# Sub-chunk outputs written from PSUM into x^T, and who issues the six small transfers

## The chip, the cores and the metric

One core of one Trainium2 chip runs the whole program. The metric is the device time of one execution in microseconds (us): the median of three runs is 731.37 us (729.12 to 733.59). Engines are called as in the profile: PE (TensorE), PEld (its weight loads), DVE (VectorE), ACT (ScalarE), POOL (GpSimd), SP (SyncE, which here only issues DMAs).

## The reference, cut to what matters

```python
def _attn_ref(r, k, v, w, u):                  # (4, 8, 768, 48): batch, heads, tokens, D
    state = np.zeros((B, H, D, D))
    for t in range(S):
        cur = np.einsum('bhd,bhe->bhde', u[None] * kt, vt)
        y[:, :, t] = np.einsum('bhd,bhde->bhe', rt, state + cur)
        state = w[None, :, :, None] * state + np.einsum('bhd,bhe->bhde', kt, vt)
    return y
x = attn_out.transpose(0, 2, 1, 3).reshape(3072, 384)
x = (np.maximum(x @ w_in, 0) ** 2) @ w_out     # 384 -> 2048 -> 384
h = x @ w2_in                                  # 384 -> 1024
# h * softmax(h), layer norm over the 1024, times g_ln, then @ w2_out (1024 -> 384)
```

## The kernel before, in words

The 3072 tokens are 24 chunks of 128, and six blocks of 512 tokens (four chunks each) go through the first two matrices. The attention is computed chunk by chunk. Chunks 0 to 3 are the first of their batch and take a direct form. Chunks 4 to 23 are worked in two sub-chunks of 64 tokens: `prep_rk`, `prep_b`, `prep_kt` scale r and k, `pe_scores` and `pe_u` multiply on PE, `dve_mask` and `dve_state` put the masked scores and the state beside v and r, and `pe_av` gives the chunk's output.

`pe_av` (L505 to L526) leaves the output in one PSUM bank as y: a pair of heads has one head in partitions 0 to 47 and the other in 64 to 111, and the four pairs lie one after another, 128 columns each. The next matrix wants x^T as three tiles of 128 full partitions. So x^T (`xr`) takes pairs 0 to 2 in the same partitions, and the fourth pair is cut into pieces of 16 rows that fill the gaps, partitions 48 to 63 and 112 to 127, of the three tiles. Before the change ACT copies all of y into the SBUF tile `ys` (L519), and SP issues eight transfers from `ys` to `xr` a chunk: two of 48 partitions by 384 columns (L524), six of 16 partitions by 128 columns (L526). `split_x` then makes a high part `xh` on ACT (L570) and a low part `xl` on DVE (L571), both float32r, of the chunk's columns of its block.

The block's work is a list of steps. `p1(i)` (L651 to L659) multiplies 128 columns of w_in with x^T, nine matmuls, and ACT applies relu, square and the rounding to `gh` (L656, L657, L658), DVE takes the remainder `gl` (L659). `p2(i)` (L669 to L673) multiplies both with w_out, nine matmuls. `p1` is written two steps ahead of `p2`; `gh` and `gl` have three buffers, and the PSUM of `p1` has two.

Chunks 4 to 7 are the second block's chunks. Their attention is put between the steps of the first block (the `side` lists), and there the weights are still being made: `w1_conv` takes a loaded piece, turns its 64-bit numbers into 32 bits on DVE (L591, L594, L597), rounds it on ACT (L609, `wih` or `woh`) and takes the remainder on POOL (L610, `wil` or `wol`), and `w1_load` asks SP for the next piece (L580, L582). The chunks from 8 on are put between the steps of the later blocks (the `ev` lists). The second network follows, token tile by token tile.

SP's queue holds, in one order, the loads of chunks (L241 to L246), the weight loads, the eight transfers a chunk, and stores. A DMA that waits holds what is behind it. The order of instructions on each engine is made by the tile scheduler, which simulates the program in time; only the small matmuls marked with `pin` keep the written order. `xr` has two buffers, `ys` one. The tag of `ys` is also used once for the table `dup` before chunk 4.

Of the kernel before, what the change touches and what calls it, by code (L numbers as in the profile page):

```python
# [8 lines left out]
F32 = mybir.dt.float32  # L9
# [7 lines left out]
B, H, S, D = 4, 8, 768, 48  # L17
NP = H // 2
DM = H * D
KD = DM // 128  # L20
NT = B * S
C = 128
# [4 lines left out]
GR = 112  # L27
# [150 lines left out]
def rwkv_moe_moe2_kernel(ctx, tc, rkd, tok, tk2, wd, w, u, w_in, w_out, w2_in, w2_out, g_ln, out):  # L178
    nc = tc.nc
# [16 lines left out]
    ap = att_ctx.enter_context(tc.tile_pool(name="ap", bufs=2))  # L196
# [212 lines left out]
    def pin(ins):  # L409

        tc.keep_in_program_order(ins)
# [94 lines left out]
    def pe_av(c, yb=2):  # L506
        rk_t.pop(c)
        tok_t.pop(c)
        y = ps[:, yb, :].rearrange("p (a i) -> p a i", a=NP)
        for s in range(2):  # L510
            i = slice(s * CH, (s + 1) * CH)
            for p in range(NP):
                for j in range(2):
                    pin(nc.tensor.matmul(  # L514
                        y[64 * j:64 * j + D, p, i], vs[c % 2][:KR[j], j, s, p], mv[c % 2][:KR[j], j, p, i],
                        start=True, stop=True,
                    ))
        ys = ap.tile([GR, NP, C], F32, tag="ys", bufs=1, name="ys")
        nc.scalar.copy(ys, y[:GR])  # L519
        xr = ap.tile([128, KD, C], F32, tag="xr", name="xr")  # L520
        xr_t[c] = xr
        for j in range(2):
            o = 64 * j
            nc.sync.dma_start(out=xr[o:o + D], in_=ys[o:o + D, 0:KD])  # L524
            for k in range(KD):
                nc.sync.dma_start(out=xr[o + D:o + 64, k], in_=ys[o + 16 * k:o + 16 * k + 16, KD])  # L526

    def pe_av_direct(c, yb=2):

# [359 lines left out]
    for q, c in enumerate(range(4, 8)):  # L889
        t = 5 + 3 * q + (q > 0)  # L890
        side[t].append(lambda c=c: (prep_rk(c), put_state(c, 0), prep_kt(c), prep_b(c)))
        side[t + 1].append(lambda c=c: (pe_u(c), pe_scores(c), dve_state(c), dve_mask(c)))
        side[t + 2].append(lambda c=c: (pe_av(c, 0), load_chunk(c + 2)))
        side[t + 3].append(lambda c=c: split_x(c))
# [20 lines left out]
    for q, t in enumerate(visits):  # L915
        c = 2 * B + q
        if q:
            ev[t].append(lambda c=c: pe_av(c - 1))
            ev[t + 2].append(lambda c=c: split_x(c - 1))
        if c < NC:  # L920
            ev[max(t - 2, first_full)].append(
                lambda c=c: (prep_rk(c), put_state(c, 0), prep_kt(c), prep_b(c))
            )
            ev[t].append(lambda c=c: (pe_u(c), pe_scores(c), dve_state(c), dve_mask(c)))
        if q and c + 1 < NC:
            ev[t].append(lambda c=c: load_chunk(c + 1))
# [114 lines left out]
```

## Time and profile before

| | |
|---|---|
| median of three runs | 731.37 us (729.12 to 733.59) |
| the profiled execution: time, span | 732.05 us, 730.3 us |
| PE busy | 702.9 us (96%) |
| DVE, ACT, POOL busy | 418.7 us (57%), 321.7 us (44%), 267.9 us (37%) |
| mean granted clock of TensorE | 0.993 |

The span is from the first to the last instruction of the profiled execution. Busy time is time in which an engine has an instruction at work; issuing DMAs and waiting for semaphores are not counted. A granted clock of 1.0 is full speed. A busy share is a mean over stages: the start, where weights are made, and the later blocks differ much.

### The profile page before, as it was taken

To read this page: it belongs to the slowest core of one execution; us is meant where nothing else is said; L and a number is where in the kernel's file an instruction comes from. 1 tells how busy PE (TensorE), PEld (TensorE's weight loads), DVE (VectorE), ACT (ScalarE), POOL (GpSimd) and SP (SyncE) were. 2 spreads that over 40 slices of the span, in tenths; PEclk is the share of its full clock that TensorE was granted. 3 is DMA by queue.
4 is the path that set the end of the run, shared out by engine and by line. 5 is a ranking of instruction groups with operands and counts; after the bars stand their busy time and mean duration, and the time that the engine had idled before them with its cause. 6 is when DMAs were issued, how large, how long until landed. Compare 5 with 4: busy or idle time off the path is not lost.

```text
span 730.3 us, 13143 instructions
## 1 busy us (share of the span) xinstructions
PE 702.9 (96%) x5088; PEld 599.7 (82%) x5088; DVE 418.7 (57%) x752; ACT 321.7 (44%) x625; POOL 267.9 (37%) x297
## 2 busy tenths in 40 slices
PE   3799999999999999999999999999999999999996
PEld 3588768788888888888888888888899999999996
DVE  7799986444534334433333266614768767777671
ACT  1444645454554554555454455634433232322232
POOL 6969777444533333334222022802303030300000
PEclk9999999999999999999999999999999999999999
DMA  8956552222312222321161016221111100000001
GB/s 277 267 200 212 140 179 79 89 67 85 106 57 89 67 66 66 108 65 60 41 202 35 12 41 202 88 86 34 66 65 49 40 22 11 22 22 22 22 34 38
DMA packets 35113, 62.73 MB, mean 86 GB/s; under 512 B 7777, under 2 KB 17378, under 8 KB 35042
## 3 DMA queue, kind: packets, MB, share of 16 engines
q1 hardware_dynamic: 35042, 61.80, 27.2%
q8 instruction: 42, 0.69, 0.4%
q14 instruction: 29, 0.24, 0.1%
HBM read 48.41 MB, written 9.44 MB: 79 GB/s over the span
## 4 chain that ended last, share of the span: by engine, by line
PE 86%; DMA 7%; SPq 2%; POOL 2%; ACT 1%; issue 1%; DVE 0%; ACTq 0%; POOLq 0%; DVEq 0%
PE ps L651 9%; PE ps L653 8%; PE ps L652 8%; PE ps L670 8%; PE ps L669 8%; PE ps L673 8%; PE ps L819 5%; PE ps L818 5%; PE ps L821 5%; PE ps L755 5%; PE ps L757 5%; PE ps L756 5%; DMA stg<-in_w_out_dram 3%; PE ps L802 3%; PE ps L514 2%; PE ps L437 2%
## 5 line engine op out<-in xcount | busy, mean ns | idle before, releaser
L659 DVE TENSOR_TENSOR gl<-ps,gh 128x512 fp32r<-128x512 f32 (+1 forms) x100 | 66.7, 668 | 168.2 <-ACT gh L658 166.9
L651 PE MATMUL ps<-xh,wih 128*128 128x512 f32 (+1 forms) x300 | 117.5, 393 | 1.8 <-ACT xh L570 1.0
L653 PE MATMUL ps<-xh,wil 128*128 128x512 f32 (+1 forms) x300 | 115.2, 385 | 2.3 <-POOL wil L610 2.3
L669 PE MATMUL ps<-gh,woh 128*128 128x512 f32 (+1 forms) x300 | 113.3, 383 | 2.2 <-ACT gh L658 2.1
L652 PE MATMUL ps<-xl,wih 128*128 128x512 f32 (+1 forms) x300 | 115.0, 384 | 0.1
L670 PE MATMUL ps<-gh,wol 128*128 128x512 f32 (+1 forms) x300 | 113.3, 383 | 0.0
L656 ACT ACTIVATE ps<-ps 128x512 f32<-128x512 f32 (+1 forms) x100 | 56.3, 564 | 115.9 <-PE ps L653 115.4
L356 POOL TENSOR_TENSOR mv<-mv,pt 48x512 f32<-48x512 f32 x40 | 52.1, 1302 | 93.0 <-DMA mv<-in_rkd_dram 92.3
L673 PE MATMUL ps<-gl,woh 128*128 128x512 f32 (+1 forms) x300 | 83.3, 382 | 0.0
L653 PEld LDWEIGHTS ps<-xh,wil 128*128 128x128 f32 x300 | 56.7, 189 | 14.3 <-POOL wil L610 3.1
L651 PEld LDWEIGHTS ps<-xh,wih 128*128 128x128 f32 x300 | 56.4, 189 | 14.5 <-ACT xh L570 1.6
L669 PEld LDWEIGHTS ps<-gh,woh 128*128 128x128 f32 x300 | 56.0, 189 | 13.9 <-ACT gh L658 2.9
L652 PEld LDWEIGHTS ps<-xl,wih 128*128 128x128 f32 x300 | 56.8, 190 | 10.8 <-DVE xl L571 0.6
L818 PE MATMUL ps<-w2oh,lth 128*128 128x384 f32 x192 | 65.1, 339 | 0.2 <-ACT lth L811 0.2
L670 PEld LDWEIGHTS ps<-gh,wol 128*128 128x128 f32 x300 | 56.1, 189 | 11.2 <-issue 0.4
L819 PE MATMUL ps<-w2ol,lth 128*128 128x384 f32 x192 | 65.2, 339 | 0.0
L673 PEld LDWEIGHTS ps<-gl,woh 128*128 128x128 f32 x300 | 55.7, 189 | 10.9
L658 ACT CAST gh<-ps 128x512 fp32r<-128x512 f32 (+1 forms) x100 | 56.9, 571 | 2.8
L657 ACT ACTIVATE ps<-ps 128x512 f32<-128x512 f32 (+1 forms) x100 | 56.4, 566 | 2.8
L755 PE MATMUL ps<-w2ih,xh 128*128 128x512 f32 x144 | 57.4, 398 | 0.0
L827 ACT COPY ob<-ps 128x384 f32<-128x384 f32 x24 | 11.5, 480 | 102.9 <-issue 81.2
L756 PE MATMUL ps<-w2il,xh 128*128 128x512 f32 x144 | 56.8, 395 | 0.0
(120 smaller groups left out, 1232.8 us busy)
## 6 DMA issues: line engine op xcount, KB each, us to landing
stg<-in_w_in_dram SPq DMA_DIRECT2D x18, 512.0 KB, 6.9
stg<-in_w_out_dram SPq DMA_DIRECT2D x24, 384.0 KB, 6.0
tok<-in_tk_dram SPq DMA_DIRECT2D x20, 384.0 KB, 3.6
x2d<-stg SPq DMA_DIRECT2D x18, 256.0 KB, 2.5
x2r<-x2d SPq DMA_DIRECT2D x6, 768.0 KB, 4.9
out_dram<-ob SPq DMA_DIRECT2D x24, 192.0 KB, 1.9
kd<-in_rkd_dram SPq DMA_DIRECT2D x20, 224.0 KB, 3.5
mv<-in_rkd_dram SPq DMA_DIRECT2D x40, 96.0 KB, 2.3
```

The lines of the kernel that those rows point to most:

```text
L651: nc.tensor.matmul(hp, wih[g][:, k, f], xh[:, k, cs], start=(k == 0), stop=False)
L652: nc.tensor.matmul(hp, wih[g][:, k, f], xl[:, k, cs], start=False, stop=False)
L653: nc.tensor.matmul(hp, wil[g][:, k, f], xh[:, k, cs], start=False, stop=(k == KD - 1))
L658: nc.scalar.copy(gh, hp)
L659: nc.vector.tensor_tensor(out=gl, in0=hp, in1=gh.bitcast(F32), op=ALU.subtract)
L669: nc.tensor.matmul(acc[e], woh[m // 4][:, m % 4, f], gh, start=start, stop=False)
L670: nc.tensor.matmul(acc[e], wol[m // 4][:, m % 4, f], gh, start=False, stop=False)
L673: nc.tensor.matmul(acc[e], woh[m // 4][:, m % 4, f], gl, start=False, stop=stop)
L755: nc.tensor.matmul(o, x2h[j][:, k, s], w2["ih"][:, k, fs], start=(k == 0), stop=False)
L756: nc.tensor.matmul(o, x2h[j][:, k, s], w2["il"][:, k, fs], start=False, stop=False)
L818: nc.tensor.matmul(o, hi[:, m], w2["oh"][:, m], start=(m == 0), stop=False)
L819: nc.tensor.matmul(o, hi[:, m], w2["ol"][m // 4][:, m % 4], start=False, stop=False)
```

## The change

Instead of copying all of y to `ys`, ACT copies the fourth pair (128 columns) to a smaller `ys`, and the first three pairs (384 columns) straight to partitions 0 to 111 of `xr`. The gap partitions 48 to 63 are written along with them, from rows of PSUM that hold nothing of use, and the transfers overwrite them. The two large transfers are gone. The six small ones stay; for chunks 4 to 7 (`c < 2 * B`) they are issued by ACT, for chunks 8 to 23 by SP as before.

```diff
-        ys = ap.tile([GR, NP, C], F32, tag="ys", bufs=1, name="ys")
-        nc.scalar.copy(ys, y[:GR])
+        ys = ap.tile([128, C], F32, tag="ys", bufs=1, name="ys")
         xr = ap.tile([128, KD, C], F32, tag="xr", name="xr")
         xr_t[c] = xr
+        nc.scalar.copy(ys[:GR], y[:GR, KD])
+        nc.scalar.copy(xr[:GR], y[:GR, :KD])
+        eng = nc.scalar if c < 2 * B else nc.sync
         for j in range(2):
             o = 64 * j
-            nc.sync.dma_start(out=xr[o:o + D], in_=ys[o:o + D, 0:KD])
             for k in range(KD):
-                nc.sync.dma_start(out=xr[o + D:o + 64, k], in_=ys[o + 16 * k:o + 16 * k + 16, KD])
+                eng.dma_start(out=xr[o + D:o + 64, k], in_=ys[o + 16 * k:o + 16 * k + 16])
```

## Rows read from the trace of the kernel before

**Rows 1.** Busy time (count) by engine in three stretches, then granted clock, DMA share, GB/s
```profile
0.00:50.00 50.00, 32.55 (x268) 27.57 (x270) 39.48 (x84) 15.22 (x33) 39.54 (x48) 0.97 0.81 251
...
76.00:135.00 59.00, 54.82 (x500) 42.85 (x499) 47.32 (x80) 31.44 (x64) 40.58 (x39) 0.97 0.50 150
135.00:700.00 565.00, 565.00 (x3881) 483.35 (x3881) 294.29 (x518) 251.19 (x480) 165.20 (x188) 1.00 0.20 62
```

**Rows 2.** PE's waits from 76 to 135 us: total, times, longest
```profile
PE ps L514 <- DVE mv L481: 1.0, 1, 1.0
PE ps L651 <- ACT xh L570: 1.0, 1, 1.0
```

**Rows 3.** Timeline of PE: start, duration, instruction, idle before it
```profile
103.39 0.50 PE L653 MATMUL ps<-xh,wil 128*128 128x512 f32 x1 [0.62 <-POOL wil L610]
104.34 0.50 PE L651 MATMUL ps<-xh,wih 128*128 128x512 f32 x1 [0.45 <-ACT wih L609]
...
105.71 0.60 PE L653 MATMUL ps<-xh,wil 128*128 128x512 f32 x1 [0.64 <-POOL wil L610]
...
106.54 0.63 PE L652 MATMUL ps<-xl,wih 128*128 128x512 f32 x1
106.97 0.63 PE L653 MATMUL ps<-xh,wil 128*128 128x512 f32 x1
...
109.70 0.40 PE L669 MATMUL ps<-gh,woh 128*128 128x512 f32 x1
109.93 0.39 PE L670 MATMUL ps<-gh,wol 128*128 128x512 f32 x1
...
125.25 0.39 PE L669 MATMUL ps<-gh,woh 128*128 128x512 f32 x1
```

**Rows 4.** Timeline of ACT, chunk 5 and chunk 7
```profile
89.68 0.57 ACT L519 COPY ys<-ps 112x512 f32<-112x512 f32 x1
...
100.76 0.52 ACT L570 CAST xh<-xr 128x384 fp32r<-128x384 f32 x1 [5.89 <-DMA xr<-ys]
...
103.63 0.65 ACT L609 CAST wih<-stg 128x512 fp32r<-128x512 f32 x1
...
120.87 0.57 ACT L519 COPY ys<-ps 112x512 f32<-112x512 f32 x1
...
122.58 0.59 ACT L658 CAST gh<-ps 128x512 fp32r<-128x512 f32 x1
...
129.65 0.51 ACT L570 CAST xh<-xr 128x384 fp32r<-128x384 f32 x1 [1.49 <-DMA xr<-ys]
```

**Rows 5.** Timeline of SP's DMA issues, chunk 5 and chunk 7
```profile
90.61 0.55 SPq L524 DMA_DIRECT2D xr<-ys  x1
92.88 3.17 SPq L526 DMA_DIRECT2D xr<-ys  x3
...
97.59 1.85 SPq L526 DMA_DIRECT2D xr<-ys  x3
...
121.67 0.55 SPq L524 DMA_DIRECT2D xr<-ys  x1
...
124.80 1.85 SPq L526 DMA_DIRECT2D xr<-ys  x3
```

**Rows 6.** The small transfers, all chunks: issue in ns; issue to landing in us
```profile
L526 SPq DMA_DIRECT2D xr<-ys x120: 507/587/1723, 79.2 to 426.3; - x120
...
DMA to landing us min/median/max: 1.7/1.8/5.1
```

**Rows 7.** ACT's short copies, by form: count, busy us, mean ns, idle before
```profile
L417 ACT COPY vs<-sg 48x192 f32<-48x192 f32 x80 | 28.1, 351 | 30.2 <-DVE sg L502 27.4 <-PE ps L514 1.5
```

**Rows 8.** Timeline of POOL from 101 us
```profile
101.66 1.68 POOL L610 TENSOR_TENSOR wil<-stg,wih 128x512 fp32r<-128x512 f32 x1
104.36 1.30 POOL L610 TENSOR_TENSOR wil<-stg,wih 128x512 fp32r<-128x512 f32 x1 [1.03 <-ACT wih L609]
```

**Rows 9.** Timeline of DVE at 100 us
```profile
100.13 0.69 DVE L597 SCALAR_TENSOR_TENSOR stg<-stg,ps 128x512 uint32<-128x512 uint32 x1
```

## The prediction

> **What bounds the kernel now.** I read the windows first. From 135 to 700 us PE is busy in 565.00 of 565.00 us at granted clock 1.00 [rows 1]: there nothing that ACT, SP or the transfers do can give time, and only a stall of PE could cost some. In the first 50 us PE idles 17.45 us (50.00 - 32.55), but no sub-chunk output exists yet: the first of the transfers is issued at 79.2 us [rows 6]. What the change can move is 76 to 135 us, where chunks 4 to 7 lie among the weight conversion: 59.00 us, PE busy 54.82, so 4.18 us idle, mean clock 0.97 [rows 1]. Next I read PE's waits and its timeline there. One cluster is 0.62 + 0.45 + 0.64 = 1.71 us at 102.8 to 105.7 us, for `wil` and `wih`, weights of `p1` [rows 3]. One is 0.98 us for the masked scores and one 0.97 us for `xh` of chunk 7 [rows 2]; some 0.5 us are crumbs. Behind the first cluster the matmuls follow each other every 0.43 us (106.54 to 106.97) where 0.23 us is the pace before and after (109.70 to 109.93): TensorE ran at the lower of its two levels, 1.2 instead of 2.4 GHz, after those idle gaps. From 105.71 to 109.70 us ten matmuls take 3.99 us instead of 10 x 0.23 = 2.30, a loss of 1.69 us [rows 3].
>
> So all that can be won is 4.18 + 1.69 = 5.87 us, 0.8% of the time.
>
> Why is the first cluster late? ACT and SP tell it. `wih` L609 starts at 103.63 because ACT, which works in order, stood 5.89 us until 100.76 for `xr` of chunk 5 [rows 4]. SP began its eight issues for that chunk at 90.61; three small ones took 3.17 us instead of 1.85, and the last ended at 99.44 (97.59 + 1.85) [rows 5]. That output had been copied at 90.25 (89.68 + 0.57) [rows 4]: 10.5 us from there to the `xh` that it feeds.
>
> **The change, part by part.**
>
> The copy. One 112x512 copy of 0.57 us [rows 4] becomes a 112x128 and a 112x384 copy, the same columns and one more start. From 0.351 us for 192 columns [rows 7] and 0.57 for 512 [rows 4] a column costs (0.57 - 0.35) / 320 = 0.0007 us and a start 0.22 (an estimate), so the two take 0.79 us, 0.22 us more a chunk; the ends are 0.57 and 1.14. For the 16 chunks from 8 on ACT has the room: it is busy 251.19 of 565 us [rows 1], so 3.5 us more in all cost nothing. If that cover were gone, a chunk would cost its 0.22 us.
>
> The two large transfers go. On SP that is 2 x 0.6 us of issue a chunk. From chunk 8 on it brings `xr` about 1.2 us forward for a PE that doesn't wait: 0. The pace there would only be hurt if `xh` came later, and it doesn't.
>
> The six small transfers of chunks 4 to 7 move to ACT. The trace has no DMA issued by ACT. The nearest row is SP's own for the same transfer: 0.587 us median (0.507 to 1.723) [rows 6], three in 1.85 us with the gaps, 0.617 each [rows 5]. I take that for ACT, 3.70 us a chunk. Bounds: 0 (ACT goes on while the issue proceeds) and 1.72 us each, 10.3 us a chunk. Four chunks are 14.8 us of ACT, which has 59.00 - 31.44 = 27.6 us idle in the stretch [rows 1]; but its work comes in order, so each time relu, square, rounding and weight casts queue behind, and PE behind those.
>
> What SP gets back: in this stretch 4 x 8 issues, some 20 us (32 x 0.617). The loads behind them, chunks' k, r, v and the next weight pieces, leave up to 5 us earlier; POOL and DVE get their data sooner. Many of these loads wait for a buffer anyway, and DVE is busy 47.32 of 59.00 us [rows 1]. I count 0 for it, between 0 and 1.6 us (0.98 for the masked scores and the 0.62 us wait for a `wil` that POOL ended at 103.34 [rows 8]).
>
> Chunk 5, the important one. Copies end at 89.68 + 0.79 = 90.47, six issues at 94.17, the last of which starts at 93.55 and lands 1.8 us later (median; 5.1 at most, and this is where the weight loads crowd) [rows 6]: 95.4 to 98.7, instead of 100.6. From `xh` to the start of `wih` ACT needs 103.63 - 100.76 = 2.87 us [rows 4], so `wih` could start at 98.3 to 101.6; but DVE hands over its input only at 100.82 (100.13 + 0.69) [rows 9]. So it starts 2.0 to 2.8 us earlier. POOL, busy with the `wil` before until 103.34, makes the next one from 103.34 to 104.64 instead of 104.36 to 105.66 [rows 8]. On PE the first wait of 0.62 us stays, the second (0.45 for `wih`) goes, and so PE comes to the third at 105.71 - 0.64 - 0.45 = 104.62 [rows 3], where the `wil` is there at 104.64. Won: 0.45 + 0.64 - 0.02 = 1.07 us. Whether the clock then stays up can't be read: bounds 0 and 1.69. I take the 1.69, since the gaps that preceded the fall shrink from 1.71 to 0.64 us, and the single gaps of 0.98 and 0.97 us of the stretch [rows 2] brought no fall: 3.99 us at half clock are 2.0 us of the (1 - 0.97) x 59 = 1.8 us that the mean clock lacks [rows 1, 3], so there was just this one. Sum 2.76 us.
>
> Chunk 7. Copies from 120.87 end at 121.66, the issues at 125.36, the landing at 126.5 or so, `xh` ready near 127.1 instead of 130.16 [rows 4]: the 0.97 us wait [rows 2] goes. But if the issues stand before the relu, square and rounding that now end at 123.17 (122.58 + 0.59) [rows 4], that `gh` comes 0.22 + 3.70 = 3.92 us later, 127.1; PE wants it at 125.25 [rows 3], the cover is 2.08 us, and 1.84 us are lost. If the scheduler puts the activations first, nothing is lost and the landing is near 129, 0.6 us gained. The term lies between -0.97 and +0.87 us; I take 0. Chunks 4 and 6 have the same two sides, with no PE wait on `xh` to win: 0, up to 1.84 each lost.
>
> A rule to weigh. Issue of a small transfer took 0.587 us against 1.8 us from issue to landing [rows 6], and landing took up to 5.1. The Trainium skill (DMA: Bandwidth & Descriptors, Issuing engines are not separate DMA queues) says that transfers issued by several engines run on the same 16 DMA engines and interleave, and that a second issuer saves only the time of issuing, usually small beside the transfer. The first half speaks against this change: ACT's six would stand among the same weight loads, and the 98.7 us of chunk 5 would be right rather than 95.4. By it the sum is the same, as DVE's 100.82 and POOL's 103.34 decide. The second half the trace does not bear out here: six issues, 3.7 us, are twice the 1.8 us of a landing.
>
> Sum: 1.07 + 1.69 = 2.76 us won. Against the profiled execution, 732.05 us (the span of 730.3 and 1.75 around it), that is 729.3; this execution lies 0.68 above the median of 731.37, and on the median's scale the forecast is 728.6 us.
>
> **The rivals.**
>
> All of it goes (chance 0.26). SP, rid of 32 issues, brings the loads early enough that POOL and DVE are no longer late, ACT's issues fall into its idle time, PE runs through from 76 to 135 us. For: POOL waits for loads and ACT for `xr` in this very stretch. Against: DVE is busy 80% of it, and that doesn't change. Time: 731.37 - 5.87 = 725.5.
>
> No net effect (0.18). ACT's 3.7 us stand where its 5.89 us wait stood; the order of work changes but the cluster of waits and the slow clock stay, or come at another place. For: ACT waits 5.89 us for chunk 5 but only 1.49 us for chunk 7 [rows 4], so elsewhere 3.7 us of issuing is more than the wait that it replaces. Time: 731.4.
>
> ACT becomes the bound (0.12), the slower side. The six issues stand in ACT's order ahead of the activations, `gh` is late, and `p2` and then `p1` (whose two PSUM buffers wait for `gl`) stand still. With the cover of 2.08 us found at chunk 7 it decides as soon as an issue costs ACT over (2.08 - 0.22) / 6 = 0.31 us and they stand first. At 0.617 a chunk loses 1.84 us; for three of four chunks, 5.5 us, less the 0.97 us wait for chunk 7: 4.6 us, so 736.0. At the upper bound of 1.72 us an issue a chunk loses 8.5 us and the time is over 750; I find no row near that as a median. Against it: ACT idles 27.6 us, and the scheduler places ACT's work by simulated times.
>
> That the change does not do what it says has no place here: the transfers are named in the code. But the scheduler may order every engine's work in the stretch anew, and this is the widest unknown.
>
> **How the numbers follow.** A change under 0.5% (3.7 us) can't be told from none by a measurement of this kernel. The forecast has 0.44, with its own range 727.0 to 731.0 (the clock loss stays or goes, chunk 7 either way). Faster by over 0.5% is below 727.7: nearly all of the rival at 725.5 and a quarter of the forecast's, 0.36. Slower by over 0.5% is above 735.0: most of the last rival, 0.10. The rest is 0.54. The range 725.2 to 733.2 reaches from the best case to half of the last rival's loss.
>
> **What would show it.** In the changed profile: ACT's wait for `xr` of chunk 5 gone or under 2 us; `wih` and `wil` of that cluster 1 to 3 us earlier, and no stretch with matmuls 0.43 us apart between 100 and 112 us; PE idle in 76 to 135 us about 3.1 us; from 135 us on PE fully busy as before. ACT's issues should show as about 0.6 us each. PE waiting for `gh` (L658) or `gl` (L659) right after each of the four copies would show the last rival. The forecast fails if PE's idle time in the stretch is the same or larger, or is nearly nil.

## The result: 0.6% slower, and the profile after

The changed kernel takes 734.68 us (median of 8 runs, 733.9 to 735.62) against 730.55 us for the kernel before on the same chip (8 runs, 729.11 to 733.59): ratio 1.0060, 95% interval 1.0042 to 1.0078. The forecast was 728.6 us. The profiled execution took 735.16 us, its span is 733.4 us, and PE is busy 703.3 us against 702.9.

Busy time by engine after the change, in the stretches of [rows 1], then in three parts of the second one, and in five microseconds of the first of these (columns as there):

```profile
0.00:50.00 50.00, 34.25 (x288) 29.31 (x289) 40.96 (x89) 17.04 (x37) 39.61 (x48) 0.97 0.81 253
76.00:135.00 59.00, 51.03 (x427) 40.30 (x426) 41.22 (x68) 27.41 (x60) 42.69 (x39) 0.94 0.40 116
135.00:700.00 565.00, 565.00 (x3937) 483.30 (x3936) 289.61 (x521) 254.81 (x500) 163.31 (x184) 1.00 0.20 61
...
85.00:100.00 15.00, 10.56 (x90) 8.48 (x91) 11.35 (x17) 7.31 (x16) 13.84 (x13) 0.77 0.51 144
100.00:112.00 12.00, 10.58 (x75) 8.49 (x74) 11.67 (x22) 7.04 (x16) 9.26 (x9) 1.00 0.40 122
112.00:135.00 23.00, 21.18 (x173) 16.51 (x172) 10.03 (x16) 10.99 (x23) 14.74 (x14) 1.00 0.17 48
...
90.00:95.00 5.00, 5.00 (x13) 3.91 (x12) 3.96 (x8) 0.98 (x3) 4.41 (x6) 0.50 0.84 234
```

The same three parts in the kernel before:

```profile
85.00:100.00 15.00, 13.59 (x142) 10.72 (x141) 14.55 (x23) 7.89 (x16) 10.10 (x11) 1.00 0.69 204
100.00:112.00 12.00, 10.29 (x68) 7.33 (x68) 9.44 (x16) 8.30 (x18) 9.91 (x10) 0.86 0.49 151
112.00:135.00 23.00, 21.94 (x233) 17.69 (x232) 14.98 (x26) 11.69 (x24) 13.67 (x14) 1.00 0.42 128
```

Set beside each other, the two fences show that the place forecast did get better: from 100 to 112 us the clock is 1.00 instead of 0.86 (0.14 x 12 = 1.7 us back) and PE idles 1.42 us instead of 1.71. But from 85 to 100 us, where the kernel before had lost little, PE is busy 3.03 us less and the mean clock is 0.77. Part of that low clock falls into time in which PE idles anyway; PE works at 0.50 from 89.44 to about 95.0 us, which costs (95.0 - 89.44) x 0.5 = 2.8 us. Over the 59 us PE is busy 3.79 us less. Idle time and work at the low clock together cost 7.97 + 2.8 = 10.8 us here and 4.18 + 1.69 = 5.9 us before: 4.9 us more. The start stretch, which the change doesn't touch, had 1.70 us more PE time in this execution than in the one of before, so 3.2 of the 4.9 remain, and the two profiled executions differ by 3.11 us. From 135 us on PE is full, as before.

PE's waits from 76 to 135 us in the changed kernel (columns as in [rows 2]), and what they are on PE's timeline:

```profile
PE ps L672 <- ACT gh L661: 4.7, 1, 4.7
PE ps L654 <- DVE gl L662: 2.0, 2, 1.4
PE ps L654 <- ACT xh L573: 1.3, 1, 1.3
```

```profile
83.61 1.10 PE L514 MATMUL ps<-mv,vs 112*48 112x64 f32 x32
89.44 0.80 PE L672 MATMUL ps<-gh,woh 128*128 128x512 f32 x1 [4.73 <-ACT gh L661]
90.03 0.63 PE L673 MATMUL ps<-gh,wol 128*128 128x512 f32 x1
...
94.30 0.63 PE L656 MATMUL ps<-xh,wil 128*128 128x512 f32 x1
...
105.00 0.50 PE L654 MATMUL ps<-xh,wih 128*128 128x512 f32 x1 [1.42 <-DVE gl L662]
```

The waits for `wil` and `wih` of [rows 3] are not among them. In their place PE stands 4.73 us for `gh`, and then matmuls follow each other every 0.43 us from 90.03 to 94.7 us: TensorE is at 1.2 instead of 2.4 GHz after the gap. The same two matmuls in the kernel before:

```profile
86.23 1.10 PE L514 MATMUL ps<-mv,vs 112*48 112x64 f32 x32 [0.98 <-DVE mv L481]
87.53 0.50 PE L669 MATMUL ps<-gh,woh 128*128 128x512 f32 x1 [0.20 <-ACT gh L658]
```

So PE came to this place 2.62 us earlier than before and left it 1.91 us later: the 4.73 us of idle time are in part a lead that it had and lost. The chain of waits up to ACT's `xh`, which stands before `gh`, tells what held them (start, duration, what):

```profile
75.89 4.72 DMA vs<-in_tk_dram
...
80.63 0.52 ACTq L529
...
81.82 3.74 DMA xr<-ys
...
85.74 0.51 ACT xh L573
```

An issue on ACT (80.63) stood until a load of `vs`, issued by SP at 75.89, had landed at 80.61. That was its last and shortest stand, 0.5 us; the longest, 3.0 us, lies before the fourth issue, which starts at 79.6, when the weight load that SP issued at 75.03 lands (4.6 us). I take the reason to be that the DMAs of SP and ACT share DMA semaphores and that such a transfer's semaphore was still in use by a load; no trace here shows the semaphores. ACT's timeline has the issues for all four chunks:

```profile
75.05 0.25 ACT L523 COPY ys<-ps 112x128 f32<-112x128 f32 x1
...
75.33 7.53 ACTq L529 DMA_DIRECT2D xr<-ys  x6
82.91 0.73 ACT L417 COPY vs<-sg 48x192 f32<-48x192 f32 x2 [7.23 <-DVE mv L481]
...
88.81 1.05 ACT L661 CAST gh<-ps 128x512 fp32r<-128x512 f32 x2
...
90.06 0.54 ACTq L529 DMA_DIRECT2D xr<-ys  x1
...
90.92 5.80 ACTq L529 DMA_DIRECT2D xr<-ys  x5
96.77 0.58 ACT L659 ACTIVATE ps<-ps 128x512 f32<-128x512 f32 x1 [5.78 <-DMA xr<-ys]
...
100.61 0.66 ACT L612 CAST wih<-stg 128x512 fp32r<-128x512 f32 x1 [2.20 <-DVE stg L600]
101.17 0.51 ACT L573 CAST xh<-xr 128x384 fp32r<-128x384 f32 x1
...
106.42 3.72 ACTq L529 DMA_DIRECT2D xr<-ys  x6
...
123.33 3.85 ACTq L529 DMA_DIRECT2D xr<-ys  x6
```

Chunk 4's six issues take from 75.33 to 82.86, and what stands behind them in ACT's order starts at 82.91: copies of `vs`, three weight pieces, `xh` (which waits for the last transfer until 85.74), the activations, and at last `gh`. (The profile puts ACT's wait of 7.23 us down to the masks on DVE; in the kernel before the same copies of `vs` run at 80.01, and those masks only from 84.66, so it was the issues.) The issues themselves, by engine (issue in ns; landing in us), and the two copies:

```profile
L529 SPq DMA_DIRECT2D xr<-ys x96: 507/585/1928, 152.3 to 427.4; - x96
L529 ACTq DMA_DIRECT2D xr<-ys x24: 514/600/1041, 75.3 to 126.6; - x24
...
DMA to landing us min/median/max: 1.6/1.8/5.0
```

```profile
L523 ACT COPY ys<-ps x20: 250/255/267, 75.1 to 424.0; 112x128 f32<-112x128 f32 x20
L524 ACT COPY xr<-ps x20: 466/472/484, 75.2 to 424.2; 112x384 f32<-112x384 f32 x20
```

### The profile page after: what moved, and what is told of

It reads as the page before. It is cut to its first block, busy times and chain, and to the rows that moved or that the text cites. A ratio compares the mean times of both kernels' runs of the same rounds, so it can differ in the third digit from the quotient of the medians.

```text
span 733.4 us, 13087 instructions
## 1 busy us (share of the span) xinstructions
PE 703.3 (96%) x5088; PEld 600.3 (82%) x5088; DVE 411.4 (56%) x752; ACT 322.4 (44%) x645; POOL 270.0 (37%) x297
## 4 chain that ended last, share of the span: by engine, by line
PE 86%; DMA 6%; DVE 2%; POOL 2%; ACT 1%; issue 1%; SPq 0%; ACTq 0%; DVEq 0%; POOLq 0%
PE ps L654 9%; PE ps L672 8%; PE ps L673 8%; PE ps L656 8%; PE ps L655 8%; PE ps L676 8%; PE ps L822 5%; PE ps L821 5%; PE ps L824 5%; PE ps L758 5%; PE ps L760 5%; PE ps L759 5%; PE ps L805 3%; PE ps L514 2%; DMA stg<-in_w_out_dram 2%; PE ps L437 2%
```

## The experiments

Three things changed at once: the copies, who issues the transfers, and, since the scheduler made everything anew, the order of instructions on every engine. Against the kernel before, the changed kernel's order differs in 32 stretches of instructions on PE, 35 on DVE, 57 on ACT, 17 on POOL and 45 on SP (counted from the orders that h6_act_loads_behind and h8_sp_afterorder are held to; on ACT and SP the change's own instructions are among them). To part these, some kernels have each engine's order held to that of another kernel, with ordering edges only (in short):

```diff
+    for e, want in HELD.items():          # engine -> its instructions in the other kernel's order
+        seq = [named[e][k] for k in want]
+        for a, b in zip(seq, seq[1:]):
+            tc.add_manual_dep(b, a.name, DependencyInfo(NoSync, DATA))
```

"New order" is the order that the scheduler made for the version with direct copies in which SP issues. Each ratio is to the kernel before in the same batch; between batches one kernel moves by some 0.2 to 0.5% (0.9975 and 1.0021; 1.0058 and 1.0039), so ratios that close are not told apart, and the last column, from one profile, is only a second witness: the same kernel showed 0.95 us of PE's wait for the masked scores in one profile (h1_sp_oldorder) and 3.08 us in another (h1b_sp_oldorder).

| kernel | issuer of chunks 4 to 7 | order | ratio to before, 95% | PE busy of 59.00, clock (76 to 135 us) |
|---|---|---|---|---|
| before | SP | - | 1 | 54.82, 0.97 |
| changed | ACT | its own | 1.0060 (1.0042 to 1.0078) | 51.03, 0.94 |
| e1_sp_all | SP | its own (new) | 1.0058 (1.0036 to 1.0081) | 53.02, 0.97 |
| e1b_sp_all | SP | new, again | 1.0039 (1.0020 to 1.0059) | 51.79, 1.00 |
| e3_act_45 | ACT for 4, 5 | its own | 1.0079 (1.0046 to 1.0111) | 52.67, 0.94 |
| e4_act_67 | ACT for 6, 7 | its own | 1.0137 (1.0109 to 1.0165) | 48.30, 0.88 |
| e5_loads_behind | ACT | its own | 1.0097 (1.0072 to 1.0122) | 50.70, 0.94 |
| h1_sp_oldorder | SP | before's | 0.9975 (0.9947 to 1.0004) | 56.38, 1.00 |
| h1b_sp_oldorder | SP | before's, again | 1.0021 (0.9999 to 1.0044) | 55.83, 0.97 |
| h2_act_oldorder | ACT | before's | 1.0124 (1.0098 to 1.0151) | 50.31, 0.91 |
| h6_act_loads_behind | ACT | before's | 1.0093 (1.0077 to 1.0109) | 50.68, 0.94 |
| h7_act7_only | ACT for 7 | before's | 1.0033 (1.0015 to 1.0052) | 54.05, 0.97 |
| h8_sp_afterorder | SP | the changed kernel's | 1.0163 (1.0138 to 1.0189) | 49.12, 0.91 |
| h4_before_e1order | SP, code of before | new | 1.0099 (1.0071 to 1.0126) | 51.74, 0.94 |
| e9_sp_late | SP | its own, split_x late | 1.0035 (1.0015 to 1.0056) | 53.34, 0.97 |
| h5_xfwd | SP | before's, xh and xl new | 1.0017 (1.0004 to 1.0029) | 55.35, 0.97 |
| h9_queue_e1 | SP | before's, SP new | 0.9997 (0.9976 to 1.0019) | 55.14, 0.97 |
| h10_three_e1 | SP | before's, DVE, ACT, POOL new | 1.0077 (1.0048 to 1.0105) | 53.06, 0.97 |
| h11_pool_e1 | SP | before's, POOL new | 1.0065 (1.0044 to 1.0086) | 55.40, 0.97 |
| h12_two_e1 | SP | before's, DVE, ACT new | 1.0030 (1.0015 to 1.0044) | 54.39, 0.97 |

**Who issues, the order left to the scheduler.** `eng` is `nc.sync` for all chunks in the first, and ACT's for two of the four chunks in the others:

```diff
-        eng = nc.scalar if c < 2 * B else nc.sync
+        eng = nc.sync                                            # e1_sp_all
+        eng = nc.scalar if c < B + 2 else nc.sync                # e3_act_45
+        eng = nc.scalar if B + 2 <= c < 2 * B else nc.sync       # e4_act_67
```

> The changed kernel, but SP issues the six small transfers for all chunks; the direct copy into xr stays. Theory A (ACT stands still while it issues, 7.5 us for chunk 4, and the activations behind it are late): no slower than the kernel before, 727 to 731.5 us, the PE wait of 4.7 us for gh is gone. Theory B (the split copy from PSUM and the gap rows written twice cost the time): about 734, as the changed kernel. Theory C (any new order of the stretch costs a few us by chance): anywhere from 729 to 736.

> ACT issues for chunks 4 and 5 alone, SP for 6 and later. Theory A with its refinement (the loss is where ACT also waits for SP's loads, that is at chunks 4 and 5, where its issues took 7.5 and 6.7 us, against 3.7 and 3.9 for chunks 6 and 7): 733 to 735, the loss of the changed kernel nearly whole. If all four chunks lose alike: 732 to 733. Theory B: about 734 as well; it is told apart by the run with SP alone.

> ACT issues for chunks 6 and 7 alone. Theory A refined: 729 to 732, ACT's issues take 3.7 us a chunk and PE loses 0 to 1.9 us over the run with SP alone. If all four chunks lose alike: 732 to 733. Theory B: about 734.

With SP issuing, the time is as long as with ACT, which theory A had ruled out. Two chunks on ACT are not half of four: 1.0079, not told apart from 1.0060, and 1.0137, clearly above it. So a sum by chunks fails, since each version has an order of its own. What they share is the wait: PE stands 4.9 us for `gh` in the one and 6.8 in the other, and with SP issuing in its own order there is none for `gh`. There PE stands for `mv` (3.4 us in the first run, 2.8 in the second) and, in the second, for `wil` (3.5 us).

**ACT's wait at the issue.** The loads of `mv` and `vs` of chunks 6 to 9 are put behind the transfers of the chunk two before, so that ACT's transfers are not issued beside those loads (the edit in short):

```diff
+            tc.add_manual_dep(load_of_chunk[c], last_transfer[c - 2], NoSync)   # 6 <= c < 10
```

> The changed kernel, with the loads of mv and vs for chunks 6 to 9 ordered behind the six transfers that ACT issues for the chunk two before, so that ACT's issues no longer wait for those loads. Theory A refined (ACT waits at its issue for an earlier transfer, the loads of SP): ACT's six issues for chunk 4 take 3.7 to 4.5 us instead of 7.5, the PE wait for gh of 4.7 us shrinks to about 1.5, the time falls to 729.5 to 732.5. If the issue itself is what blocks ACT and not what it waits for: still 6 us and more, and 734. Against it: the loads leave 2 to 4 us later, which may cost some of it.

The four groups of issues take 3.79, 3.88, 3.82 and 3.88 us now; chunk 4's had taken 7.53. That agrees with the reading that the issues had waited for loads. But the time did not fall (1.0097): PE waits 5.9 us for `gh`, 2.09 us at the place of the 4.73 and 3.81 us at chunk 6. So the wait at the issue isn't needed for the loss. That the issues alone make it is not shown here: the order is again the scheduler's own, and between chunk 4's issues and that `gh` ACT also waits 1.23 us for DVE and 1.21 us for a transfer.

**Issuer and order apart.** Direct copies in the order of before, with SP issuing (twice) and with ACT issuing; the latter again with the loads behind (the same order on all engines; only which earlier transfer an issue waits for differs); then ACT for chunk 7 alone:

> The direct copy with SP issuing all small transfers, but with every engine's instructions held to the order of the kernel before (the second copy stands right behind the first, the six transfers where six of the eight stood). Theory D (the cost is in the new order that the scheduler makes: xh and xl of a sub-chunk come earlier on ACT and DVE than their transfers land, and the masks and activations behind them wait): no slower than the kernel before, 727.5 to 731.5 us, and no PE wait of 3 us for the masked scores. Theory B (the split copy and the direct write themselves cost it): 734 to 736, as with SP alone in the scheduler's own order.

> The same kernel as the run with the direct copy, SP issuing and the old order, run again for a narrower interval, as it is the only one so far that may beat the kernel before: ratio 0.994 to 1.000, 726.5 to 731 us.

> The changed kernel as it is, ACT issuing for chunks 4 to 7, but every engine's order held to that of the kernel before, ACT's transfers right behind its copies. Theory D alone: as the kernel before or up to 3 us faster, 727.5 to 731.5 us. Theory A (ACT stands still while it issues): 733 to 738 even so, with PE waiting for gh after chunks 4 and 5. Both at work: about 732.

> ACT issues for chunks 4 to 7, every engine in the order of the kernel before, and the loads of mv and vs for chunks 6 to 9 counted behind ACT's transfers, so that these get other DMA semaphores: the order on all five engines is the same as in the run with ACT issuing in the old order, only which earlier transfer an issue waits for differs. If ACT's wait at the semaphore is the cost: ACT's six issues take 3.7 to 3.9 us for chunk 4 instead of 7.2, and the time falls from a ratio of 1.012 to 1.000 to 1.006. If the 3.7 us of plain issuing are the cost: still 1.009 to 1.014.

> Old order held, SP issues for all chunks but chunk 7, whose six transfers ACT issues, at a place where no weight piece stands behind them. Plain issuing delays the two or three activations behind it by 3.7 us, of which 2.1 us are covered: a loss of 0 to 2 us against SP alone in the old order, ratio to the kernel before 0.997 to 1.002. If issuing on ACT costs nothing by itself: 0.994 to 0.998.

With every engine in the order of before, SP issuing makes no difference that can be told (0.9975, 1.0021), and ACT issuing costs 1.5% (1.0124 over 0.9975 in one batch) or, with the loads behind, 0.7% (1.0093 over 1.0021 in another). The first pair differs in the issuer alone. The loads that are put behind leave later, which may cost something by itself; no run has them behind with SP issuing. First SP's, then ACT's window, and PE's waits with ACT:

```profile
76.00:135.00 59.00, 56.38 (x523) 44.77 (x519) 51.06 (x83) 34.57 (x74) 46.17 (x43) 1.00 0.46 140
```

```profile
76.00:135.00 59.00, 50.31 (x473) 40.40 (x473) 43.51 (x72) 27.75 (x62) 42.04 (x40) 0.91 0.39 116
```

```profile
PE ps L681 <- DVE mv L632: 4.7, 1, 4.7
PE ps L821 <- DVE gl L829: 4.0, 1, 4.0
```

ACT's first six issues take 7.24 us there, and the copies of `vs`, the weight pieces and the activations are late behind them. One chunk on ACT (h7_act7_only) is the smallest case. Its time, 1.0033, isn't told apart from SP alone in the same batch (1.0021); what it shows is the wait. ACT's timeline, then PE's:

```profile
121.09 3.80 ACTq L697 DMA_DIRECT2D xr<-ys  x6
124.93 0.58 ACT L833 ACTIVATE ps<-ps 128x512 f32<-128x512 f32 x1 [3.87 <-DMA xr<-ys]
...
126.16 0.58 ACT L835 CAST gh<-ps 128x512 fp32r<-128x512 f32 x1
```

```profile
126.80 0.50 PE L846 MATMUL ps<-gh,woh 128*128 128x512 f32 x1 [1.81 <-ACT gh L835]
```

Six issues in 3.80 us, relu, square and rounding behind them, and PE idle for 1.81 us on `gh`. The rival on the slower side had 1.84 us for this chunk.

**The fourth corner: SP issuing in the changed kernel's order.**

> The direct copies, SP issues all transfers, but PE, DVE, ACT and POOL are held to the order that they have in the changed kernel, and SP's queue too (the six transfers of chunks 4 to 7 put where SP has them in its own-order version). With the old order held, SP issuing measured 0.9975 and 1.0021, ACT issuing 1.0124 and 1.0093; the changed kernel measured 1.006. Theory A, the issuing on ACT alone makes it slower: here ACT issues nothing, so 1.000 (0.998 to 1.002) and PE busy over 55 us of the 59 from 76 to 135 us. Theory B, the new order costs as much by itself: 1.005 or more, PE busy 51 to 53 us. If both count, 1.002 to 1.005.

1.0163, worse than the changed kernel itself. That is above "1.005 or more", but neither theory had an order that costs SP more than ACT. Each order fits its issuer: SP in before's order 1.000 and in the changed kernel's 1.0163, ACT in before's 1.0124 and in the changed kernel's 1.0060. In the changed kernel SP issues the load of `tok` at 80.18 us; here six transfers stand before it in SP's queue (78.17 to 82.64), it leaves at 84.00, and what the order has put behind it on POOL and DVE waits with it. (Where the transfers stand in SP's queue was my choice, after the own-order version.) So issuer and order can't be added as two shares of the 0.6%.

This run also tells what the 4.73 us at `gh` are made of, since it has the changed kernel's order and no issue on ACT. ACT's copy for chunk 4 and the next `gh` here, and PE's wait; then ACT's two in the kernel before:

```profile
75.90 0.26 ACT L690 COPY ys<-ps 112x128 f32<-112x128 f32 x1
...
87.74 1.05 ACT L834 CAST gh<-ps 128x512 fp32r<-128x512 f32 x2
```

```profile
88.37 0.49 PE L845 MATMUL ps<-gh,woh 128*128 128x512 f32 x1 [2.57 <-ACT gh L834]
```

```profile
76.39 0.58 ACT L519 COPY ys<-ps 112x512 f32<-112x512 f32 x1
...
86.89 0.59 ACT L658 CAST gh<-ps 128x512 fp32r<-128x512 f32 x1
```

PE waits 2.57 us for this `gh` even so. From the copy to `gh` it is 10.50 us before, 11.84 us here, and 13.76 us in the changed kernel (75.05 to 88.81). So of the 3.26 us by which `gh` comes later, 1.34 go with the new order and 1.92 with ACT's issuing, as far as one profile each can tell, and with SP's queue not the same in the two.

**What in the new order costs, with SP issuing.** The code of before in the new order; `split_x` of chunks 4 to 6 pinned behind the next chunk's masks; then the order of before with parts of the new one. The line that moves `split_x`:

```diff
-        side[t + 3].append(lambda c=c: split_x(c))
+        side[t + 3 if c == 7 else 5 + 3 * (q + 1) + 1 + 2].append(lambda c=c: split_x(c))   # e9_sp_late
```

> The kernel before, one copy and eight transfers by SP, with every engine's order held to the one that the scheduler made for the direct copy with SP issuing. Theory D: as slow as that one or slower, 734 to 738 us, with PE waiting 3 us and more for the masked scores, since the transfers now land later still. Theory B: as the kernel before, 729.5 to 731.5.

> Direct copy, SP issues for all chunks, and split_x of chunks 4 to 6 is written behind the masks of the chunk after, its two instructions kept in the written order, so that neither ACT nor DVE can meet a transfer that has not landed ahead of the masks. Theory D: 727.5 to 731 us, ACT and DVE no longer wait for xr of chunks 4 to 6, PE's wait for the masked scores under 1 us. Theory B: still 734 and more. If it is chance of order (theory C): anywhere from 729 to 736 with other waits.

> The direct copy with SP issuing, every engine held to the order of the kernel before, except that xh (ACT) and xl (DVE) of chunks 4 to 7, eight instructions, stand where the scheduler put them for the direct copy: xl of chunk 4 ahead of a weight piece and of the masks of chunk 5, xl of chunk 5 between two masks, and so on. Theory D (these early places, with the transfers not landed, are what costs): 733 to 736, ratio 1.003 to 1.008, DVE waits for xh and PE for the masked scores, some 3 us at 83 to 88 us. If it is the rest of the order (masks, weights, activations changed places among themselves): as with the old order whole, 0.995 to 1.001.

> SP issues, every engine held to the order of the kernel before, only SP's own queue (loads, transfers) as in the own-order version that measured 1.0058. If the place of the loads in SP's queue makes that version slow: 1.004 to 1.006, and POOL or DVE waits for a load in 76 to 135 us. If the order on the computing engines does: 1.000 (0.998 to 1.002).

> The other half: DVE, ACT and POOL ordered as in the own-order version, PE and SP as in the kernel before. If the order on DVE, ACT and POOL makes that version slow: 1.004 to 1.006 and PE busy under 54 us from 76 to 135 us. If it is the queue of SP, or only PE's and SP's order together with it: 1.000 (0.998 to 1.002).

> The own-order version with SP issuing, again, beside the three held ones: both theories say what it measured, 1.0058 (1.0036 to 1.0081); if it comes out at 1.000 to 1.002 there is nothing in the order to explain, and the whole loss of the changed kernel is ACT's issuing.

The code of before loses 1% in the new order, so the order costs by itself. With `split_x` late PE no longer waits for the masked scores, but 5.6 us for `wil`, and the time is 1.0035, not the 727 to 731 us of theory D. I had taken the place of `xh` and `xl` for the cause, as in the new order `xl` of chunk 4 stands before the masks on DVE. That fell: with only these moved the time is 1.0017, beside 1.0021 for the same without it. SP's queue is not the cause either (0.9997). The three elementwise engines together are (1.0077), and two runs part them:

> SP issues, every engine held to the order of the kernel before, only POOL ordered as in the own-order version. The three elementwise engines together measured 1.0077, with PE waits of 2.8 us for wil (made at 107.15, behind kd and tok on POOL) and 2.2 us for mv (masked scores behind xl on DVE). If POOL's order is the cause: 1.003 to 1.006 and the wait for wil of 2 us or more is here. If not: 0.998 to 1.002.

> The other part: DVE and ACT ordered as in the own-order version, POOL, PE and SP as in the kernel before. If DVE's and ACT's order is the cause (xl ahead of the masks and of a weight piece, and the weight conversion after it): 1.004 to 1.008, with the wait for mv of 2 us or more. If POOL's is: 0.998 to 1.002. If both lose a part, 1.002 to 1.005 here and there.

POOL's order alone costs 1.0065, DVE's and ACT's 1.0030. POOL's timeline in before's order (h1_sp_oldorder) and in the new one (h11_pool_e1), and PE's with the latter:

```profile
102.53 1.30 POOL L780 TENSOR_TENSOR wil<-stg,wih 128x512 fp32r<-128x512 f32 x1 [1.10 <-ACT wih L779]
```

```profile
101.62 1.28 POOL L508 TENSOR_TENSOR mv<-mv,pt 48x512 f32<-48x512 f32 x1
104.13 1.28 POOL L503 TENSOR_TENSOR kd<-kd,pt 112x512 f32<-112x512 f32 x1 [1.23 <-PE ps L682]
105.37 0.99 POOL L537 TENSOR_TENSOR tok<-tok,ub 128x384 f32<-128x384 f32 x1
106.32 1.29 POOL L787 TENSOR_TENSOR wil<-stg,wih 128x512 fp32r<-128x512 f32 x1
```

```profile
107.66 0.50 PE L830 MATMUL ps<-xh,wil 128*128 128x512 f32 x1 [2.36 <-POOL wil L787]
```

In the new order POOL scales `mv`, `kd` and `tok` of the next chunk before it makes the last `wil`, `kd` has to wait for PE, and `wil` ends at 107.61 instead of 103.83: PE stands 2.36 us. Behind this gap the clock is 0.65 from 107.6 to 112 us, some 1.5 us more (0.35 x 4.4). Together that is 3.9 of the 4.7 us by which this kernel is slower than before. But the kernel before has its own cluster of waits and slow clock, PE's other waits here are shorter than there, and h9_queue_e1, with before's order on POOL and no loss of time, shows 2.0 us of wait for `wil` as well. So one profile does not give the account, and why POOL's order costs 0.65% is only argued. The changed kernel has another order of POOL, with no such wait: this part belongs to the version with SP issuing, not to the changed kernel's 0.6%.

No version beats the kernel before beyond doubt.

## Why the prediction was wrong

**What bounds the kernel** held: PE is full from 135 us on, and all that moved lies in 76 to 135 us.

**Chunk 5's cluster** came in part as forecast. The waits for `wih` and `wil` went, the last `wih` starts at 100.61, when DVE hands it over (2.0 to 2.8 us earlier were forecast, it is 3.02), and the clock stayed up from 100 to 112 us (1.7 us, the forecast's 1.69). The way there was another one, so this was luck in part: `xh` of chunk 5 starts at 101.17, later than before [rows 4], since ACT's last issue ends at 96.72, and `wih` is early because the scheduler has put it before `xh`. And in the same stretch PE stands 1.42 us for `gl`, so of the 1.07 us of idle time 0.29 were won.

**The copies** were right: 0.255 + 0.472 = 0.73 us where 0.79 was estimated, covered from chunk 8 on.

**The price of an issue on ACT** was right for the issue, 0.600 us where 0.617 was taken. The sum was not: 14.8 us for four chunks were 7.53 + 0.54 + 5.80 + 3.72 + 3.85 = 21.44 us, because issues on ACT waited, at chunk 4 for SP's loads to land. With this wait away (e5_loads_behind, h6_act_loads_behind) the loss stayed, so it isn't the step that decides.

**The step that failed** is "Chunks 4 and 6 have the same two sides, with no PE wait on `xh` to win: 0, up to 1.84 each lost", together with "The term lies between -0.97 and +0.87 us; I take 0" for chunk 7. I set 14.8 us of issuing against 27.6 us of ACT's idle time and let the scheduler find room. At chunk 4 there was no room before the next `gh`: PE stood 4.73 us for it and then worked 5.6 us at half clock, a loss of 2.8 us. The bound of 1.84 us was too low for three reasons: the issues took 7.53 us instead of 3.70; the new order makes this `gh` late by itself (PE waits 2.57 us for it in h8_sp_afterorder, with no issue on ACT); and the gap brought the slow clock, whose price stood in the forecast for the cluster that goes and not for a gap that comes. At chunk 7 of the changed kernel PE waits 1.26 us for `xh`, where 0.97 was to be won at best. The Trainium skill (DMA: Bandwidth & Descriptors, Issuing engines are not separate DMA queues) says that a second issuing engine saves only the time of issuing, usually small beside the transfer. Here that time is not small beside the transfer, six issues of 0.600 us against 1.8 us to landing, and freeing SP of 32 issues won nothing that shows in the time.

The stated range, 725.2 to 733.2 us, doesn't follow from its own two terms, which give 725.5 and 731.37 + 2.3 = 733.7; 734.68 lies outside both.

**The rival "ACT becomes the bound"** had the mechanism (PE waiting for `gh` and `gl` behind the issues), its size at one chunk (1.84 us forecast, 1.81 measured in h7_act7_only) and nearly the time (736.0 against 734.68). That its time came so near is luck in part: it counted 1.84 us at three of four chunks, and the trace has one large wait, at chunk 4, with a slow clock that it did not count. Its chance of 0.12 was too small: its own text said that it decides from 0.31 us an issue, the nearest row had 0.587, and only ACT's idle share and the scheduler's placing stood against it.

**The new order**, named as the widest unknown and not priced, costs or gives as much as the change: the code of before is 1% slower in the order made for another version, direct copies with SP issuing are 0.4 to 0.6% slower than the kernel before in the scheduler's order and no slower in before's, and the changed code measured 1.0124 in before's order against 1.0060 in its own. That issuing on ACT costs time is shown with the order held, and so is that the order does with the issuer held. How much of the 0.6% is the issuer's and how much the order's stays open, as the two don't add.

## What to carry to other kernels

A DMA that is moved to a computing engine is priced at its issue time times the number of them, and whatever the issue waits for, set before the next result that the bottleneck waits for on that engine, not against the engine's idle share; with a cover of 2.08 us six issues of 0.6 us don't fit. The scheduler, which orders by simulated times, answered this small edit with a new order on every engine. A change of 0.5% could be read only with the order held, and the order made for one issuer was a bad one for the other. A gap of the bottleneck is priced with the slow clock that may follow it: 2.8 us behind the 4.73 us here.

## What was not expected of the hardware

An issue on ACT waited for a load that SP had issued: six issues took 7.53 us beside SP's loads in flight and 3.79 us with those loads behind (e5_loads_behind). The issue itself costs ACT as much as SP, 0.600 against 0.585 us in the median, and ACT's next work starts only behind the group (82.91, 96.77, 110.19 and 127.22 us after groups that end at 82.86, 96.72, 110.14 and 127.18). A PE gap of 4.73 us was followed by 4.7 us of matmuls at half the rate, while gaps of 1.42 and 1.26 us later in the same execution were not (clock 1.00 from 100 to 135 us).
